# Norm products ahead of the last scores, and one exp for each block of columns, in the opening of an attention and feed-forward kernel

## Chip, cores, metric

The kernel runs on one core of a Trainium2 chip. The metric is device time in microseconds (us) of one execution, as a median over executions. "Before" is the tuned kernel, "after" the changed one. A trace is one execution taken by the hardware profiler; its span is about 2 us shorter than the device time.

## The reference, cut to what matters

```python
# q, k, v: [4, 6016, 256];  x is [24064, 256];  tau = 1
qn = q / (norm(q, axis=1) + 1e-6)          # norms over the 6016 tokens, one per column
kn = k / (norm(k, axis=1) + 1e-6)
s  = kn.T @ qn / tau                       # [256, 256] for each of 4 batches
a  = exp(s - rowmax);  a /= a.sum(-1) + 1e-9
x  = v @ a
out = (sigmoid(x @ w_gate) * (x @ w_val)) @ w_out      # 256 -> 1536 -> 256
```

## The kernel before

`v @ a` is never formed. For each batch the kernel folds the 256x256 attention matrix into the weights (`G = a @ w_gate`, `H = a @ w_val`, called the gate and val products below, twelve groups of two matmuls) and then runs a long main loop of matmuls over tokens. For batches 1 to 3 the norms and scores are worked out inside the main loop of the batch before. Batch 0 has nothing to hide behind: its path runs in the first 40 us. It is the only part that the change touches.

```python
def norms_sqrt(b):                 # ScalarE: square root of the summed squares, 128x4
def norms_inv(b):                  # VectorE: add 1e-6, reciprocal
def spread_k(b, i, pl, tag):       # TensorE: k's inverse norms along the free axis, in PSUM
def copy_s(b, j):                  # VectorE: scores from PSUM to SBUF, 128x256, for j = 0, 1

def weights(b, i):                 # block i of 128 columns
    ...
    for j in range(CB):            # CB = 2
        y = attp.tile([P, P], FP32, tag=f"y{i}{j}", name="y_sb")
        nc.vector.tensor_tensor(
            out=y, in0=s["x"][:, j, ds(i * P, P)], in1=s["rk"][i], op=ALU.mult
        )
        nc.scalar.activation(
            out=e[:, j, :], in_=y, func=ACT.Exp, bias=shift, scale=s["r"][:, j : j + 1]
        )
    ...
# ---- the opening, after the loop over the groups of q and k ----
st[0]["n"] = ps_n0
norms_sqrt(0)
nc.scalar.preload_act_table(ACT.Exp)
copy_s(0, 0)
norms_inv(0)
copy_s(0, 1)
busy(3)
spread_k(0, 0, pso, "o")
spread_k(0, 1, pso, "o")
...
weights(0, 0)
weights(0, 1)
...                                # v of the first tokens transposed by TensorE
sums(0, 0)                         # row sums of block 0, and their inverse
gh(0, 0, psg, "g", act=False)      # gate product of block 0
gh(0, 1, psv, "v", act=True)       # val product of block 0: first reader of the first val tile
sums(0, 1, pss, "s")
gh(0, 2, psg, "g", act=False)      # gate product of block 1
gh(0, 3, psv, "v", act=True)       # val product of block 1
nc.scalar.preload_act_table(ACT.Sigmoid)
gh(0, 4, pso, "o", act=False)
# ---- the main loop, first tokens ----
            for f in range(FC):
                glu(b, ci, f)
                ...
                if (b, ci) == (0, 0) and f < len(gh_order) - 5:
                    gh(0, 5 + f, pso, "o")     # f = 2 gives the eighth product
```

`gh(b, n, pool, tag, act)` takes a PSUM buffer of the pool, runs the two matmuls, and has ScalarE (`act` true, or even `n` where it isn't given) or VectorE empty it.

Of the kernel before, what the change touches and what calls it, by code (L numbers as in the profile page):

```python
# [9 lines left out]
FP32 = mybir.dt.float32  # L10
BF16 = mybir.dt.bfloat16
ACT = mybir.ActivationFunctionType
ALU = mybir.AluOpType
# [4 lines left out]
def kernel(  # L18
# [20 lines left out]
    nc = tc.nc  # L39
    P = nc.NUM_PARTITIONS  # L40
# [8 lines left out]
    CB = C // P  # L49
# [16 lines left out]
    def pool(name, bufs, **kw):  # L66
        return ctx.enter_context(tc.tile_pool(name=name, bufs=bufs, **kw))
# [4 lines left out]
    attp = pool("attp", 1)  # L72
# [14 lines left out]
    def mm(out, lhsT, rhs, start, stop, **kw):  # L87
        nc.tensor.matmul(out, lhsT=lhsT, rhs=rhs, start=start, stop=stop, **kw)  # L88
# [21 lines left out]
    t0, nt = groups0[0]  # L110
# [15 lines left out]
    shift = consts.tile([P, 1], FP32)  # L126
# [10 lines left out]
    for fg in range(NFG):  # L137
        for w, src in enumerate((moe_w_gate, moe_w_val)):
            nc.gpsimd.dma_start(
                out=w_sb[w][fg],  # L140
                in_=src.rearrange("(t p) f -> p t f", p=P)[:, :, ds(fg * FG, FG)],
# [11 lines left out]
    def score(b, t0, u):  # L153
        q_sb, k_sb = qk[b, t0]
        if t0 == 0 and u == 0:
            st.setdefault(b, {})["s"] = pss.tile([P, CB, C], FP32, tag="s", name="ps_s")
        ps_s = st[b]["s"]
        t = t0 + u
        for j in range(CB):
            mm(  # L160
                ps_s[:, j, :],
                q_sb[:, u, ds(j * P, P)],
                k_sb[:, u, :],
                start=(t == 0 and j == 0),
                stop=(t == NT - 1),
                skip_group_check=True,
            )

    def squares(b, t0, nt, which, engine, sq=None):
        src = qk[b, t0][which]  # L170
        if sq is None:
            sq = sqpool.tile([P, TPC, C], BF16, tag=f"sq{which}", name=f"sq{which}")
        if engine is nc.scalar:
            nc.scalar.activation(out=sq[:, :nt, :], in_=src[:, :nt, :], func=ACT.Square)  # L174
        else:
            engine.tensor_tensor(  # L176
                out=sq[:, :nt, :], in0=src[:, :nt, :], in1=src[:, :nt, :], op=ALU.mult
            )
        return sq

    def norm_mms(ps, sqs, nt, first, last, order=(0, 1)):

        for w in order:
            sq = sqs[w]
            for u in range(nt):
                for j in range(CB):
                    mm(
                        ps[:, w * CB + j : w * CB + j + 1],
                        sq[:, u, ds(j * P, P)],
                        ones_bf[:, 0:1],  # L190
                        start=(first and w == order[0] and u == 0 and j == 0),
                        stop=(last and u == nt - 1),
                        skip_group_check=True,
                    )
# [80 lines left out]
    def norms_sqrt(b):  # L275
        s = st[b]
        s["r"] = attp.tile([P, 2 * CB], FP32, tag="r", name="r")
        nc.scalar.activation(out=s["r"], in_=s["n"], func=ACT.Sqrt)

    def norms_inv(b):  # L280
        r = st[b]["r"]
        nc.vector.tensor_scalar(out=r, in0=r, scalar1=1e-6, scalar2=None, op0=ALU.add)
        nc.vector.reciprocal(r, r)
        if inv_tau != 1.0:
            nc.vector.tensor_scalar(
                out=r[:, :CB], in0=r[:, :CB], scalar1=inv_tau, scalar2=None, op0=ALU.mult
            )
# [8 lines left out]
    def copy_s(b, j):  # L296
        s = st[b]
        if j == 0:
            s["x"] = attp.tile([P, CB, C], FP32, tag="x", name="x_sb")
        nc.vector.tensor_copy(out=s["x"][:, j, :], in_=s["s"][:, j, :])  # L300

    def weights(b, i):

        s = st[b]
        e = attp.tile([P, CB, P], BF16, tag=f"e{i}", name=f"e_sb{i}", bufs=2)
        for j in range(CB):
            y = attp.tile([P, P], FP32, tag=f"y{i}{j}", name="y_sb")
            nc.vector.tensor_tensor(
                out=y, in0=s["x"][:, j, ds(i * P, P)], in1=s["rk"][i], op=ALU.mult
            )  # L310
            nc.scalar.activation(  # L311
                out=e[:, j, :], in_=y, func=ACT.Exp, bias=shift, scale=s["r"][:, j : j + 1]
            )
        s.setdefault("e", []).append(e)
        s.setdefault("rrow", [])

# [152 lines left out]
    def busy(n):  # L469

        ps = psg.tile([P, CH], FP32, tag="g", name="ps_busy")
        for _ in range(n):
            mm(ps, ones_bf, ones_wide, True, True)

    busy(9)
    ps_n0 = psm.tile([P, 2 * CB], FP32, tag="m", name="ps_n")
# [4 lines left out]
    last0 = len(groups0) - 1  # L481
    for g, (t0, nt) in enumerate(groups0):
        engines = (nc.vector, nc.scalar) if g < last0 else (nc.scalar, nc.vector)
        sq = [squares(0, t0, nt, w, engines[w], acc[w] if g == 0 else None) for w in range(2)]
        if 0 < g < n_acc:
            for w in range(2):
                nc.vector.tensor_tensor(out=acc[w], in0=acc[w], in1=sq[w], op=ALU.add)  # L487
        for u in range(nt):
            score(0, t0, u)
        if g < n_acc:  # L490
            busy(5)
        elif g == n_acc:
            norm_mms(ps_n0, acc, TPC, True, False)
            norm_mms(ps_n0, sq, nt, False, False)
        elif nt == TPC:
            busy(2)
            norm_mms(ps_n0, sq, nt, False, False)
        elif g < last0:
            held = (sq, nt)
        else:  # L500
            norm_mms(ps_n0, *held, False, False)
            norm_mms(ps_n0, sq, nt, False, True, (1, 0))
    st[0]["n"] = ps_n0
    norms_sqrt(0)
    nc.scalar.preload_act_table(ACT.Exp)
    copy_s(0, 0)
    norms_inv(0)
    copy_s(0, 1)
    busy(3)
    spread_k(0, 0, pso, "o")  # L510
    spread_k(0, 1, pso, "o")
    busy(1)
    weights(0, 0)
    weights(0, 1)
    late = []
    transpose_v(
# [123 lines left out]
```

## Time and profile before

| | before |
|---|---|
| device time, median of three | 830.18 us (829.69 to 830.32) |
| span of the trace | 827.9 us |
| TensorE busy | 817.6 us, 99% |
| the opening up to the first val product | 37.31 us |
| of it, what the prediction took the edit to touch | 33.17 to 37.31 us |

Read it from the top down: the busy shares name the engine, the chain that ended last says where its few idle microseconds are, and the rows in order of time say what it waits for there. The lines themselves are in the prediction.

### The profile page before, as it was taken

Reading aid. Unit: us, or ns where it says so; the run is one execution under the profiler, and the core shown is the slowest. Engines: PE = TensorE matmul, PEld = TensorE weight load, DVE = VectorE, ACT = ScalarE, POOL = GpSimd, SP = SyncE. Lnnn points to the kernel's source line nnn. Section 1 sums busy time; section 2 is a strip of 40 time slices with the busy share of each in tenths; the row PEclk is TensorE's granted clock in tenths of the full one; section 3 lists DMA queues with packets and bytes.
Section 4 is the critical chain, followed back from the end, with each engine's and each line's share of the span. In section 5 each row is a group of like instructions: output and inputs, shape, how many; then the busy total and the mean of one; then the engine's idle time right before and its main releaser. Section 6 shows DMA issues by size and latency. Waiting matters only on the chain.

```text
span 827.9 us, 13794 instructions
## 1 busy us (share of the span) xinstructions
PE 817.6 (99%) x5204; PEld 503.5 (61%) x5218; DVE 588.7 (71%) x1023; ACT 391.7 (47%) x644; POOL 83.1 (10%) x159
## 2 busy tenths in 40 slices
PE   8899999999999999999999999999999999999998
PEld 4556666665665666665575666666566566666666
DVE  6577877787667777778767777777766666666665
ACT  4654444446644444445654444444655444444442
POOL 5532100002110100000311010000000000000000
PEclk9999999999999999999999999999999999999999
DMA  9999623226846433233875352223323423322111
GB/s 210 206 202 212 112 52 90 59 54 136 154 93 118 96 89 61 53 52 87 155 139 128 81 106 57 51 64 74 64 62 63 71 52 86 68 49 70 45 36 72
DMA packets 79027, 77.19 MB, mean 93 GB/s; under 512 B 50800, under 2 KB 55920, under 8 KB 78960
## 3 DMA queue, kind: packets, MB, share of 16 engines
q0 software_dynamic: 23920, 38.81, 28.1%
q1 hardware_dynamic: 54752, 36.91, 17.6%
q8 instruction: 41, 0.67, 0.3%
q10 hardware_dynamic: 288, 0.59, 0.2%
q14 instruction: 26, 0.21, 0.1%
HBM read 78.64 MB, written 24.64 MB: 125 GB/s over the span
## 4 chain that ended last, share of the span: by engine, by line
PE 94%; DMA 4%; DVE 1%; issue 0%; POOL 0%; ACT 0%; POOLq 0%
PE ps_o L88 30%; PE ps_gate L88 29%; PE ps_val L88 29%; PE ps_s L88 4%; DMA q_sb<-in_q_dram 3%; PE ps_gh L88 2%; DMA w_val<-in_moe_w_val_dram 1%; DVE hT L424 0%; DVE sq L176 0%; PE ps_end L88 0%; ACT g_sb L423 0%; PE ps_n L88 0%; POOL k_sb L97 0%; POOL q_sb L97 0%; PE ps_tp L394 0%
## 5 line engine op out<-in xcount | busy, mean ns | idle before, releaser
L424 DVE TENSOR_TENSOR hT<-ps_val,g_sb 128x512 bf16<-128x512 f32 (+1 forms) x576 | 390.7, 679 | 205.6 <-ACT g_sb L423 201.0
L423 ACT ACTIVATE g_sb<-ps_gate 128x512 bf16<-128x512 f32 (+1 forms) x576 | 338.3, 588 | 386.0 <-PE ps_gate L88 379.7
L88 PE MATMUL ps_gate<-vT,gh_G 128*128 128x512 bf16 (+1 forms) x1152 | 337.7, 375 | 0.2
L88 PE MATMUL ps_val<-vT,gh_H 128*128 128x512 bf16 (+1 forms) x1152 | 337.5, 375 | 0.3
L88 PE MATMUL ps_o<-w_out_sb,hT 128*128 128x256 bf16 x2244 | 324.9, 273 | 0.0
L88 PEld LDWEIGHTS <-hT 128*128 128x128 bf16 x2268 | 221.0, 98 | 124.6
L88 PEld LDWEIGHTS <-gh_H 128*128 128x128 bf16 x1152 | 112.7, 98 | 131.6 <-issue 1.0
L88 PEld LDWEIGHTS <-gh_G 128*128 128x128 bf16 x1152 | 112.4, 98 | 37.8 <-DVE gh_G L379 0.4
L106 POOL DMA_DIRECT2D v_sb<-in_v_dram x48 | 25.6, 533 | 619.7 <-DMA vT<-v_sb 498.5
L450 DVE COPY out_sb<-ps_o 128x256 f32<-128x256 f32 x187 | 77.2, 413 | 12.6 <-PE ps_o L88 12.6
L88 PE MATMUL ps_s<-k_sb,q_sb 128*128 128x256 bf16 x376 | 67.0, 276 | 3.9 <-DMA k_sb<-in_k_dram 2.7
L88 PEld LDWEIGHTS <-q_sb 128*128 128x128 bf16 x376 | 37.1, 99 | 12.7 <-issue 5.0
L215 DVE TENSOR_TENSOR acc<-acc,sq 128x1024 bf16<-128x1024 bf16 (+1 forms) x66 | 44.1, 669 | 0.0
L176 DVE TENSOR_TENSOR sq<-q_sb 128x1024 bf16<-128x1024 bf16 (+2 forms) x44 | 29.3, 667 | 2.7 <-DMA q_sb<-in_q_dram 2.7
L97 POOL DMA_DIRECT2D k_sb<-in_k_dram x48 | 26.2, 545 | 17.1 <-DMA k_sb<-in_k_dram 8.1
L97 POOL DMA_DIRECT2D q_sb<-in_q_dram x48 | 26.3, 548 | 14.9 <-DMA q_sb<-in_q_dram 7.4
L176 DVE TENSOR_TENSOR sq<-k_sb 128x1024 bf16<-128x1024 bf16 (+2 forms) x34 | 22.4, 658 | 0.9 <-ACT sq L174 0.9
L88 PE MATMUL ps_busy<-ones_wide,ones_bf 128*128 128x512 bf16 x57 | 17.7, 440 | 1.7 <-DVE shift L127 1.6
L174 ACT ACTIVATE sq<-k_sb 128x1024 bf16<-128x1024 bf16 (+1 forms) x11 | 11.2, 1018 | 14.5 <-DMA k_sb<-in_k_dram 13.1
L487 DVE TENSOR_TENSOR acc<-acc,sq 128x1024 bf16<-128x1024 bf16 x16 | 11.1, 691 | 5.5 <-ACT sq L174 5.2
L88 PE MATMUL ps_gh<-w_val,e_sb 128*128 128x512 bf16 x44 | 13.4, 379 | 0.2
L88 PEld LDWEIGHTS <-e_sb 128*128 128x128 bf16 x112 | 10.2, 98 | 4.7 <-ACT e_sb L311 0.5
(67 smaller groups left out, 133.8 us busy)
## 6 DMA issues: line engine op xcount, KB each, us to landing
out_dram<-out_sb SPq DMA_DIRECT2D x44, 512.0 KB, 2.9
v_sb<-in_v_dram POOLq DMA_DIRECT2D x44, 256.0 KB, 3.8
q_sb<-in_q_dram POOLq DMA_DIRECT2D x43, 256.0 KB, 7.3
k_sb<-in_k_dram POOLq DMA_DIRECT2D x43, 256.0 KB, 8.0
out_dram<-out_sb SPq DMA_DIRECT2D x3, 384.0 KB, 2.5
w_gate<-in_moe_w_gate_dram POOLq DMA_DIRECT2D x3, 256.0 KB, 6.8
w_val<-in_moe_w_val_dram POOLq DMA_DIRECT2D x3, 256.0 KB, 7.4
w_out_sb<-in_moe_w_out_dram POOLq DMA_DIRECT2D x1, 768.0 KB, 12.7
```

The costliest lines, as they stand in the source:

```text
L88: nc.tensor.matmul(out, lhsT=lhsT, rhs=rhs, start=start, stop=stop, **kw)
L97: nc.gpsimd.dma_start(out=tl[:, :nt, :], in_=rows(src, b)[:, t0 : t0 + nt, :])
L106: nc.gpsimd.dma_start(out=v_sb[:, :nt, :], in_=rows(v, b)[:, t0 : t0 + nt, :])
L174: nc.scalar.activation(out=sq[:, :nt, :], in_=src[:, :nt, :], func=ACT.Square)
L176: engine.tensor_tensor(out=sq[:, :nt, :], in0=src[:, :nt, :], in1=src[:, :nt, :], op=ALU.mult)
L215: nc.vector.tensor_tensor(out=acc[:, :nt, :], in0=acc[:, :nt, :], in1=st[b]["sq", w][:, :nt, :], op=ALU.add)
L423: nc.scalar.activation(out=g_sb[:, :n], in_=ps_gate[:, :n], func=ACT.Sigmoid)
L424: nc.vector.tensor_tensor(out=hts[b, ci][:, f, :n], in0=ps_val[:, :n], in1=g_sb[:, :n], op=ALU.mult)
L450: nc.vector.tensor_copy(out=out_sb[:, s, :], in_=ps)
L487: nc.vector.tensor_tensor(out=acc[w], in0=acc[w], in1=sq[w], op=ALU.add)
```

## The change

Three small edits, meant to shorten the latency of batch 0. Its last norm products go ahead of its last scores, so the square root can start earlier. VectorE multiplies by both inverse norms in one pass, so that the exps need no scale of their own and one exp serves a block of 256 columns instead of two of 128. The inversion goes ahead of the first copy of the scores.

```diff
@@ weights
+        y = attp.tile([P, CB, P], FP32, tag=f"y{i}", name="y_sb")
         for j in range(CB):
-            y = attp.tile([P, P], FP32, tag=f"y{i}{j}", name="y_sb")
-            nc.vector.tensor_tensor(
-                out=y, in0=s["x"][:, j, ds(i * P, P)], in1=s["rk"][i], op=ALU.mult
-            )
-            nc.scalar.activation(
-                out=e[:, j, :], in_=y, func=ACT.Exp, bias=shift, scale=s["r"][:, j : j + 1]
-            )
+            nc.vector.scalar_tensor_tensor(
+                out=y[:, j, :],
+                in0=s["x"][:, j, ds(i * P, P)],
+                scalar=s["r"][:, j : j + 1],
+                in1=s["rk"][i],
+                op0=ALU.mult,
+                op1=ALU.mult,
+            )
+        nc.scalar.activation(out=e, in_=y, func=ACT.Exp, bias=shift)
@@ the loop over the groups of q and k
+        if g == last0:
+            norm_mms(ps_n0, *held, False, False)
+            norm_mms(ps_n0, sq, nt, False, True, (1, 0))
         for u in range(nt):
             score(0, t0, u)
 ...
-        else:
-            norm_mms(ps_n0, *held, False, False)
-            norm_mms(ps_n0, sq, nt, False, True, (1, 0))
@@ after the loop
+    norms_inv(0)
     copy_s(0, 0)
-    norms_inv(0)
     copy_s(0, 1)
```

## The prediction

> **What bounds the kernel now.** I read the page first: engines, then the chain that ended last.
>
> ```profile
> PE 817.6 (99%) x5204; PEld 503.5 (61%) x5218; DVE 588.7 (71%) x1023; ACT 391.7 (47%) x644; POOL 83.1 (10%) x159
> PE 94%; DMA 4%; DVE 1%; issue 0%; POOL 0%; ACT 0%; POOLq 0%
> ```
>
> TensorE is busy for 817.6 of 827.9 us and is 94% of the chain. The rest is mostly DMA, in the opening. The edited function runs once, for the first batch; later batches use another path, which the diff leaves alone. So I cut the span at the place where the edit works (columns: stretch, its length, then busy time and instructions of PE, PEld, DVE, ACT, POOL, the granted clock, DMA share, GB/s):
>
> ```profile
> 33.17:37.31 4.14, 3.72 (x45) 2.50 (x43) 2.93 (x12) 3.54 (x8) 3.51 (x5) 1.00 1.23 203
> 37.31:50.00 12.69, 12.64 (x59) 5.55 (x60) 9.76 (x18) 9.84 (x17) 4.17 (x8) 1.00 1.27 205
> ```
>
> Everything that the edit touches begins and ends in the 4.14 us of the first row. From 37.31 us on TensorE is dense again. Even if that whole stretch vanished, the gain would be 4.14/828 = 0.5%: a change of over 2% is out of reach by size alone.
>
> Next, the chain of waits in order of time, between 30 and 43 us (start, length, what):
>
> ```profile
> 30.47 6.80 DMA w_val<-in_moe_w_val_dram
> 37.27 0.04 issue
> 37.31 0.59 PE ps_gh L88 x2
> ...
> 42.39 0.43 PE ps_val L88 x2
> 42.83 0.51 PE ps_gh L88 x2
> ```
>
> The chain does not pass through the norms, the copies or the exps. It comes out of the load of the first val-weight tile, issued at 30.47 us and landed at 37.27, and enters TensorE at 37.31 with the product that reads that tile. Last, the same stretch instruction by instruction:
>
> ```profile
> 33.42 0.40 ACT L174 ACTIVATE sq<-q_sb 128x256 bf16<-128x256 bf16 x1
> 33.57 0.29 DVE L176 TENSOR_TENSOR sq<-k_sb 128x256 bf16<-128x256 bf16 x1 [0.87 <-ACT sq L174]
> 33.84 0.44 PE L88 MATMUL ps_n<-ones_bf,sq 128*128 128x1 bf16 x12
> 34.04 0.42 DVE L300 COPY x_sb<-ps_s 128x256 f32<-128x256 f32 x1 [0.18 <-PE ps_s L88]
> 34.32 0.17 ACT L278 ACTIVATE r<-ps_n 128x4 f32<-128x4 f32 x1 [0.50 <-PE ps_n L88]
> 34.53 0.17 DVE L282 TENSOR_SCALAR r<-r 128x4 f32<-128x4 f32 x1
> 34.73 0.18 DVE L283 RECIPROCAL r<-r 128x4 f32<-128x4 f32 x1
> 34.83 0.39 DVE L300 COPY x_sb<-ps_s 128x256 f32<-128x256 f32 x1
> 35.55 0.88 DVE L308 TENSOR_TENSOR y_sb<-x_sb,ps_rk 128x128 f32<-128x128 f32 x4 [0.33 <-PE ps_rk L88]
> 35.88 1.65 ACT L311 ACTIVATE e_sb<-y_sb,shift,r 128x128 bf16<-128x128 f32 x4
> 36.81 0.18 PE L88 MATMUL ps_r<-ones_bf,e_sb 128*128 128x1 bf16 x1 [0.21 <-ACT e_sb L311]
> 36.85 0.38 PE L88 MATMUL ps_gh<-w_gate,e_sb 128*128 128x512 bf16 x1
> 41.48 0.69 DVE L424 TENSOR_TENSOR hT<-ps_val,g_sb 128x512 bf16<-128x512 f32 x1 [1.45 <-ACT g_sb L423]
> ```
>
> Two gate products stand between 36.85 and the val product (the row shows one, a record may be missing); the products of 128x512 follow one another every 0.216 us in the dense part, so TensorE reaches the val product at 36.85 + 0.43 = 37.28 anyway. The load landed at 37.27. Latency chain and load arrive together, which is why the list of waits has no row for this load.
>
> **What the Trainium skill says.** (1) "ScalarE: Activation LUTs", section What ACT_TABLE_LOAD costs: an activation with a per-partition pointer as bias takes 280 ns + 0.833 ns per element, each further pointer operand adds 93 ns. For the present exps (128 columns, bias and scale) that gives 480 ns; the trace has a median of 478. Without the scale and with 256 columns it gives 493 ns; the later batches' exps of just that shape have 500. The trace agrees. (2) "VectorE: DVE Perf Modes", section on the TRN2 errata: a float32 two-tensor operation takes (N+151)/0.96 ns, 291 ns at 128 columns; the trace has 280. The page has no row for the fused form with a scalar, so I take that from the trace. (3) "Perfetto Trace Analysis", section Per-instruction lifecycle: VectorE and ScalarE are strict first-in first-out. That matters for the reordered copies: a copy behind the inversion can no longer use the time in which the inversion waits.
>
> **The change part by part.**
>
> *Norm products ahead of the last two scores.* Now 12 norm products follow 6 score products. The scores come every 0.112 us or so, and the last two take 0.22. In the new order the 8 held norm products can start at about 33.62. The last four must still wait for the last squares, whose VectorE part ends at 33.57 + 0.29 = 33.86; with some 0.06 us of signal they start at 33.92. Products of one column follow every 0.026 us here (the 12 span 0.44, one lasts 0.163: 0.28/11), so the last starts near 34.03 instead of 33.84 + 0.28 = 34.12. Gain at the square root: 0.09 us, not 0.22.
>
> *Inversion ahead of both copies.* Before, the first copy (34.04 to 34.46) filled the wait for the square root, and the inversion began at 34.53 only because the root ended at 34.49: the copy delayed nothing. After, both copies stand behind it. Inversion 34.44, reciprocal 34.64, first copy 34.74, second 35.13 (0.39 us each from the rows of L300), first product 35.52. The spread norms, which set 35.55 before, would be there at 35.55-0.09 = 35.46. So the 0.09 shrinks to 0.03.
>
> *One VectorE pass with both norms.* Four two-tensor operations follow one another every 0.20 us (35.55 to 36.15). The fused form is in the trace at 128x256: 474 ns each, a pair in 0.86 us, so one every 0.39. Taking off 128 columns at 0.96 GHz (0.133) gives estimates of 0.34 us for one and 0.26 us apart. Added: 4 x 0.06 = 0.24 us of VectorE time.
>
> *Two exps in place of four.* Old: starts every 0.39 us from 35.88; first block of columns complete at 36.27 + 0.48 = 36.75, second at 37.53. New, with the first product at 35.52: products 0 and 1 done at 35.52 + 0.26 + 0.34 = 36.12, exp from 36.17 to 36.67; products 2 and 3 done at 35.52 + 0.78 + 0.34 = 36.64, exp from 36.69 to 37.19. The first block comes 0.08 us earlier, the second 0.34 us; ScalarE is saved two instructions.
>
> *What reaches TensorE.* The first row sum and gate product start at 36.77 instead of 36.85; then the val product comes due at 37.20 and its tile lands at 37.27. It starts at 37.31, as before. The second block is wanted only after it, so its 0.34 us go into idle time. On VectorE the first eviction of G moves 0.08 us earlier, and with it the second, on which the first gate product of the main loop waits about 0.13 us at 39.3. That 0.08 us would be won, but at 42.74 TensorE already waits about 0.08 us for a VectorE eviction, which stands behind the row at 41.48, which stands behind a sigmoid at 40.85, the sigmoid table load at 39.55 and ScalarE's eviction of the second val block at 38.85, and that follows from 37.31. An earlier TensorE just waits longer there. Sum: 0.09 - 0.06 + 0.05 = 0.08 us on the first block, 0 to 0.08 us on the end, most likely 0.
>
> **The rivals.** *The load is no pin.* The load and the chain meet within 0.02 us, so I can't see which holds; landing times are inferred. If the tile were early, the val product would move by 0.08, the second block's 0.34 us would still be cut by TensorE's own order, and the end would move by about 0.1 to 0.3 us: 829.9. Against it speaks that the chain leads back to this very load. *The copies become the bound.* If the fused form or the copies are slower by 0.1 us each, the first block comes 0.3 to 0.5 us later, past the load, and TensorE pays it: 830.4 to 830.6. For it speaks that the margin is only 0.1 us and that VectorE keeps strict order; against it, that both durations are taken from rows of this trace. *A shift that alters the steady state.* A start moved by 0.1 us could change how the 46 transposing loads or buffer releases interlock later; for this speaks that POOL spends 498.5 us in total waiting for them. But the work after 50 us is the same instructions in the same order (the lists of the two programs differ on TensorE only around the last scores), and TensorE is 99% busy there: below 0.5 us either way.
>
> **Range and chances.** Centre: 830.2 - 0.04 = 830.1 us. The three runs of before spread over 0.63 us (829.69 to 830.32), more than any effect named. I take that spread to either side and some for another chip: 829.2 to 831.0. Chances: 0.3% faster by over 2%, 99.4% within, 0.3% slower; the 4.14 us bound is what makes the middle nearly certain.
>
> **What would show it.** Right: the val product again at 37.3 us, with TensorE now idle just before it for about 0.1 us and the load named as releaser; two exps of about 500 ns, the second ending near 37.2; the square root near 34.23; the first product of norms near 35.5, with the second copy and no longer the spread norms just ahead of it; everything from 45 us on at the same times to 0.1 us. Wrong in a step: a square root still at 34.3 (the squares were the limit), a fused product starting after 35.65 (the copies bind), or a val product before 37.2 or after 37.4. My prediction fails if the time moves by more than about 1 us, which no path that I found allows.

## The result, and the profile after

After: median 830.02 us (829.89 to 830.65, six runs). Before, with the runs of the same rounds: 829.94 us (829.69 to 830.32, six runs). The ratio is 1.0002, with a 95% interval of 0.9989 to 1.0015: the same. Ratios here are the mean time of one kernel's fast runs over that of the other's fast runs of the same rounds, so not quite the ratio of the quoted medians. Experiments with one time only have no ratio, and the state of such a run is unknown; their verdicts rest on the trace.

The page of after, engines and the chain that ended last, then the two stretches that the prediction cut out (same columns):

```profile
PE 816.0 (99%) x5204; PEld 502.8 (61%) x5218; DVE 589.5 (71%) x1023; ACT 391.0 (47%) x642; POOL 83.0 (10%) x159
PE 94%; DMA 4%; DVE 1%; ACT 0%; issue 0%; POOL 0%; POOLq 0%
```

```profile
33.17:37.31 4.14, 3.58 (x45) 2.52 (x43) 3.05 (x12) 3.33 (x7) 3.53 (x5) 1.00 1.23 203
37.31:50.00 12.69, 12.55 (x58) 5.44 (x58) 9.61 (x17) 9.28 (x15) 4.14 (x8) 1.00 1.26 205
```

ScalarE has two instructions fewer; nothing else on the page tells the kernels apart (TensorE's busy time is 817.6 and 816.9 us in the two traces of before, 816.0 and 818.1 in those of after). The rows of after in order of time do (start, length, engine, operation, in square brackets the idle time ahead of it and what ended it):

```profile
33.59 0.29 DVE L176 TENSOR_TENSOR sq<-k_sb 128x256 bf16<-128x256 bf16 x1 [0.87 <-ACT sq L174]
34.05 0.38 PE L88 MATMUL ps_s<-k_sb,q_sb 128*128 128x256 bf16 x2
34.23 0.17 ACT L278 ACTIVATE r<-ps_n 128x4 f32<-128x4 f32 x1 [0.39 <-PE ps_n L88]
34.44 0.17 DVE L282 TENSOR_SCALAR r<-r 128x4 f32<-128x4 f32 x1 [0.55 <-ACT r L278]
34.73 0.73 DVE L300 COPY x_sb<-ps_s 128x256 f32<-128x256 f32 x2
35.46 1.12 DVE L308 SCALAR_TENSOR_TENSOR y_sb<-x_sb,r,ps_rk 128x128 f32<-128x128 f32 x4
36.10 1.02 ACT L316 ACTIVATE e_sb<-y_sb,shift 128x256 bf16<-128x256 f32 x2 [0.40 <-DVE y_sb L308]
36.73 0.38 PE L88 MATMUL ps_gh<-w_gate,e_sb 128*128 128x512 bf16 x1
37.33 0.59 PE L88 MATMUL ps_gh<-w_val,e_sb 128*128 128x512 bf16 x2 [0.23 <-DMA w_val<-in_moe_w_val_dram]
```

The root is 0.09 us earlier than before, the first gate product 0.12 us. The second block of columns is complete at 36.10 + 1.02 = 37.12 instead of 37.53. All of it stops at the last row: TensorE now idles ahead of the first val product, until its load has landed, and starts it at 37.33 instead of 37.31. That is the wait that the prediction named. What follows it was not foreseen. The chain of waits of after, in order of time:

```profile
30.49 6.80 DMA w_val<-in_moe_w_val_dram
37.29 0.04 issue
37.33 0.59 PE ps_gh L88 x2
...
38.87 0.69 ACT gh_H L380
...
39.58 1.28 ACT L530
...
40.87 0.61 ACT g_sb L426
...
42.11 0.75 DVE gh_G L382
42.86 0.04 issue
42.90 0.59 PE ps_gh L88 x2
```

Before, the chain stayed on TensorE between 37.31 and 43 us. After, it leaves TensorE: ScalarE's eviction of a val product, the load of the sigmoid table, the first sigmoid, a VectorE eviction, and only then TensorE's eighth product, at 42.90 instead of 42.74.

Absolute times of different executions can't be compared to 0.1 us here: the loads of q and k shift the whole opening. VectorE's last squares (the first row above) start anywhere between 33.57 and 33.96 us in the fourteen traces. From there on the same kernel, traced twice, repeats to 0.01 us up to the main loop and 0.02 us at the end. So all traces are read from that row's start:

| us after the start of the last squares | first gate product | first val product | eighth product | first output product | last 24 products ("last group") |
|---|---|---|---|---|---|
| before | 3.28 | 3.74 | 9.17 | 20.42 | 789.61 |
| after | 3.14 | 3.74 | 9.31 | 20.57 | 789.69 |

The change wins 0.14 us up to the first gate product, loses all of it at the load, and loses another 0.15 us between there and the first output product. Half of that is made up later, near 608 us, for a reason that stays open (below).

### The profile page after: what moved, and what is told of

It is laid out like the page before. It is cut to its first block, busy times and chain, and to the rows that moved or that the text cites. A ratio compares the mean times of both kernels' runs of the same rounds, so it can differ in the third digit from the quotient of the medians.

```text
span 827.8 us, 13793 instructions
## 1 busy us (share of the span) xinstructions
PE 816.0 (99%) x5204; PEld 502.8 (61%) x5218; DVE 589.5 (71%) x1023; ACT 391.0 (47%) x642; POOL 83.0 (10%) x159
## 4 chain that ended last, share of the span: by engine, by line
PE 94%; DMA 4%; DVE 1%; ACT 0%; issue 0%; POOL 0%; POOLq 0%
PE ps_o L88 30%; PE ps_gate L88 29%; PE ps_val L88 29%; PE ps_s L88 4%; DMA q_sb<-in_q_dram 3%; PE ps_gh L88 2%; DMA w_val<-in_moe_w_val_dram 1%; DVE hT L427 0%; ACT g_sb L426 0%; DVE sq L176 0%; PE ps_end L88 0%; ACT L530 0%; PE ps_n L88 0%; DVE gh_G L382 0%; ACT gh_H L380 0%
```

## The experiments

Theory: two things hide the gain. The load of the first val tile pins the first val product (A). The build gave the eighth product the other of the two PSUM buffers of the pool `pso`, which VectorE empties later than ScalarE emptied the old one (B). Rivals: the releaser that the trace names is wrong; the loss comes from the earlier norms, or is noise.

The evidence for B ahead of the runs. Rows of before, then of after, around the eighth product:

```profile
42.00 0.69 ACT L377 ACTIVATE gh_H<-ps_gh,rrow 128x512 bf16<-128x512 f32 x1
42.09 0.74 DVE L379 TENSOR_SCALAR gh_G<-ps_gh,rrow 128x512 bf16<-128x512 f32 x1
...
42.74 0.59 PE L88 MATMUL ps_gh<-w_val,e_sb 128*128 128x512 bf16 x2
```

```profile
41.90 0.69 ACT L380 ACTIVATE gh_H<-ps_gh,rrow 128x512 bf16<-128x512 f32 x1
42.11 0.74 DVE L382 TENSOR_SCALAR gh_G<-ps_gh,rrow 128x512 bf16<-128x512 f32 x1
...
42.90 0.59 PE L88 MATMUL ps_gh<-w_val,e_sb 128*128 128x512 bf16 x2
```

Before, the product starts 0.05 us after ScalarE's eviction ends (42.69) and ahead of the end of VectorE's (42.83). After, ScalarE is done at 42.59 and the product still waits until 0.05 us after VectorE's end (42.85). In the lists of the two built programs the products around the eighth come in the same order, but the eighth has another wait:

```
before:  Matmult ps_gh<-w_val_181,e_sb_509 128x512 [waits Activation_49]
after:   Matmult ps_gh<-w_val_181,e_sb_507 128x512 [waits DVE_49]
```

These lists are not among the files of the runs; the two programs, built again from their kernel.py, have the same two waits. They also show the buffers: before, the eighth product gets the one that the seventh has just used, which ScalarE empties; after, it gets that of the sixth, which VectorE empties. The products behind it swap buffers, and some waits, accordingly.

### The two kernels once more

No edit.

> The kernel before once more, for the repeatability of the trace. Counted from VectorE's last squares: first val product 3.74, eighth product 9.17, first output product 20.42, last product group 789.61, all to 0.03 us (the last to 0.1). If they scatter by 0.15 us, the difference of 0.15 us between the two kernels in these readings is noise.

> The changed kernel once more: val product 3.74, eighth product 9.31, first output product 20.57, last group 789.69, to 0.03 us (the last to 0.1). If the eighth product is at 9.1 here, the loss through the buffer was an accident of one execution.

Measured, in the order of the table's columns: 3.27, 3.73, 9.17, 20.42, 789.61 for before; 3.13, 3.73, 9.30, 20.56, 789.67 for after. Single times were 829.82 and 830.29 us. The loads were at different places (last squares at 33.67 and 33.95), and the differences stay. So 0.13 to 0.14 us at the eighth product is a property of the two programs, not of an execution, though it drowns in the spread of the device times.

### The load taken away (results wrong)

```diff
-                w_sb[w][fg][:, j, :],
+                w_sb[0 if fg == 0 else w][fg][:, j, :],
```

The first two val products read the gate tile, which is there. The load itself is still made.

> The kernel before, with the first two val products reading the gate tile, so the load of the first val tile no longer holds them (wrong result on purpose). Theory 'the load is the pin': here the chain of latencies and the load met within 0.03 us, so almost nothing is won: first val product near 37.28 us instead of 37.31, eighth product of that group still near 42.7, the end the same to 0.1 us. Rival 'the load is no pin': no different either; this run is the base for the next.

> The changed kernel with the same wrong read. Theory 'the load is the pin': TensorE no longer idles 0.23 us, the first val product starts at 36.73 + 0.43 = 37.16 instead of 37.33, so 0.12 us ahead of the run before; the sigmoid table load and the eviction behind it move up by the same 0.17, the eighth product to about 42.73. Rival 'the trace's releaser is wrong and something else holds the val product': it stays at 37.3. Time within 0.2 us of the changed kernel either way, which rounds can't show.

The former val product started two matmuls (0.43 us) behind the first gate product in both: at 3.71 in the run of before (3.74 with the load) and at 3.56 in that of after (3.74). In the absolute times that the expectation used, 37.40 and 37.20; the last squares began 0.12 and 0.05 us later here than in the first traces. So the load held before by 0.03 us and after by 0.18, as expected. The chain of the run of after no longer goes through a load; it passes through the very steps that the change shortened:

```profile
35.51 0.61 DVE y_sb L308 x2
36.12 0.02 issue
36.15 0.52 ACT e_sb L316
...
36.91 0.89 PE ps_gh L88 x4
```

The eighth product of the run of after starts at 9.14, which is the 42.73 of the expectation. First output product: 20.43 and 20.39. Here the change is worth 0.04 us, although B is still there. Times: 829.79 us, ratio 0.9999 against before, and 830.20 us, ratio 1.0004 (interval 0.999 to 1.0017), which tell nothing, as expected.

### The eighth product in a third buffer

```diff
-                    gh(0, 5 + f, pso, "o")
+                    gh(0, 5 + f, *((pss, "s") if f == 2 else (pso, "o")))
```

`pss` has one buffer, free at that time.

> The kernel before, with the eighth product of the opening group in a third, free PSUM buffer. Theory 'which buffer it gets decides when it starts' : before, it waited for ScalarE's eviction that ends at 42.69; freed of that it starts when TensorE gets there, 42.23 + 0.43 = 42.66 instead of 42.74, so 0.08 us earlier, and what follows likewise. Rival 'TensorE is held there by something other than the buffer': stays at 42.74.

> The changed kernel with the same third buffer. Theory 'the change moved the eighth product to the buffer that VectorE evicts, whose copy ends at 42.85': it starts at 42.24 + 0.43 = 42.67 instead of 42.90, and the first output product and the end come 0.2 us earlier than in the changed kernel; against slot_before no difference beyond 0.05 us, so the change proper is worth nothing. Rival 'the 0.16 us lost there comes from the later waits of the main loop or is trace noise': 42.9 stays. Time 829.8, not separable from 830.0 by rounds.

The eighth product started at 9.10 in the run of before (9.17 without the edit) and at 9.08 in that of after (9.31), where 42.66 and 42.67 of the expectations are 9.09 and 9.08; the first output product at 20.36 and 20.33, the last group at 789.55 and 789.45. The edit is worth 0.07 us to before and 0.23 us to after, and with it the two kernels are 0.03 us apart. That settles B: which buffer the eighth product gets decides when it starts, and without that the change proper is worth almost nothing. The times, 830.04 and 829.70 us (ratios 1.0002 and 0.9999, intervals of about 0.0013 either way), order the two as the traces do but show no difference.

### Part by part

Each of these is before with only the named parts of the diff; no further edit.

> Only the norm products move ahead of the last scores; copies, inversion and exps as before. All times counted from the start of VectorE's last squares, since the loads shift the whole opening by up to 0.4 us between executions. Theory 'the reordering of the copies had to come with it': the first copy now waits for scores that end at 0.84, the inversion behind it starts near 1.24 instead of 0.96, the first product of norms at 2.26 instead of 1.98, the first gate product at 3.56, and that is past the load: first val product at 4.00 instead of 3.74, first output product of the main loop at 20.68 instead of 20.42. Rival 'moving the norm products is a gain by itself': val product at 3.74, output at 20.4.

Measured: root at 0.64, inversion at 1.22, first product of norms at 2.23, first gate product 3.53, val product 3.96, first output product 20.67; one time, 830.33 us. Moving the norm products alone costs 0.22 us at the val product, because VectorE takes its instructions in order and the first copy, ahead of the inversion, now waits for scores that come later: the root ended at 34.69 us of that trace, the copy began at 34.76, and the inversion behind it only at 35.10. The inversion had to move with them.

> Norm products and inversion moved, the four products and four exps as before. Theory: root at 0.64, first product of norms at 1.87, first gate product at 1.87 + 1.30 = 3.17, val product held by its load at 3.74. The eighth product keeps the buffer that ScalarE empties (the program lists show it), so it starts at 9.08 to 9.10, not at 9.31, and the first output product at 20.33 to 20.36: a little ahead of the kernel before (20.42) and 0.2 ahead of the whole change (20.57). Rival 'the lost 0.15 us came from the earlier norms': output at 20.57 here too.

Measured: root 0.64, first product of norms 1.87, first gate product 3.16, val product 3.74, eighth product 9.08, first output product 20.34, last group 789.46; one time, 829.74 us. These two parts keep the buffer that ScalarE empties. At the first output product they are 0.08 us ahead of before and 0.23 ahead of the whole change.

> Only the fused product and the two exps; order of norms, copies and inversion as before. Theory: first product of norms at 1.98, first gate product at 1.98 + 1.27 = 3.25, val product at 3.74; the eighth product has the buffer that VectorE empties and starts at 9.31, first output product 20.57, as with the whole change. Rival 'the loss belongs to the norms': 9.17 and 20.42.

Measured: first product of norms 1.98, first gate product 3.25, val product 3.72, eighth product 9.30, first output product 20.55; one time, 830.48 us. The fused product and the single exps bring 0.03 us at the first gate product, and they alone bring the other buffer: this is the part of the diff with which the 0.15 us are lost.

### How much slack the load leaves

```diff
+    pad = attp.tile([P, C], FP32, tag="pad", name="pad")
+    for _ in range(3):
+        nc.vector.tensor_tensor(out=pad, in0=st[0]["x"][:, 0, :], in1=st[0]["x"][:, 1, :], op=ALU.mult)
     weights(0, 0)
```

> The changed kernel with three needless VectorE products of 128x256 ahead of the products of norms, about 0.34 us each, 1.0 us in all (results stay right). Theory 'the load leaves 0.15 us of slack and no more': first gate product at 3.14 + 1.0 = 4.15, val product 0.44 behind it at 4.59 instead of 3.74, and this 0.85 us is paid in full to the end: output at 21.42, time near 830.9. Rival 'the opening has more slack than the trace shows': output moves by less than 0.5 us.

The three products took 0.43 us each and started 0.46 us apart, where the expectation had 0.34: each began only after the one before had ended (they write one tile, which would explain it; not tested). The products of norms began at 3.16 instead of 1.87, 1.29 us later. The val product came at 4.85 instead of 3.74, the first output product at 21.68 instead of 20.57, the last group at 790.80 instead of 789.69: 1.11 us later in all three. So 0.18 us of a delay goes into the wait for the load, and the rest is paid one for one to the end of the kernel. The time was 831.09 us, ratio 1.0015 (0.9998 to 1.0032). The size of the delay was mis-stated in the expectation, its law was not. The 0.18 us agree with the run without the load, from the other side.

### Both holds taken away

The edits of the two sections on the load and on the third buffer together, on after.

> The changed kernel with both holds taken away: first two val products read the gate tile (wrong on purpose), eighth product in a third buffer. Theory 'load and buffer are all that hides the gain': first output product at 20.33 - 0.17 = 20.16, that is 0.26 us ahead of the kernel before. Rival 'a further wait follows': it stays at 20.3.

First output product at 20.21, last group at 789.33; one time, 829.90 us. Of the 0.26 us expected against before, 0.21 came. The trace shows two further waits. The fifth product, first reader of the second gate tile, starts at 5.01 where TensorE would have been there at 4.91; it starts at 5.01 in the run of after without the load and in the next section's version too, which fits a landing of that tile, though no run takes this load away. Then the second matmul of the main loop's first gate product is 0.06 us late, behind a VectorE eviction.

### A version that beats both

Cut here: `gh` is split into the product and `evict`, and the list `held_gh` is made.

```diff
+    nc.scalar.preload_act_table(ACT.Sigmoid)   # was after the fourth product
     sums(0, 0)
-    gh(0, 0, psg, "g", act=False)
-    gh(0, 1, psv, "v", act=True)
+    gh(0, 0, psg, "g", act=False, late=held_gh)   # its eviction is issued after sums(0, 1)
     sums(0, 1, pss, "s")
+    evict(0, *held_gh.pop())
     gh(0, 2, psg, "g", act=False)
+    gh(0, 1, psv, "v", act=False)
     gh(0, 3, psv, "v", act=True)
-    nc.scalar.preload_act_table(ACT.Sigmoid)
-    gh(0, 4, pso, "o", act=False)
+    gh(0, 4, pso, "o", act=True)
+    gh(0, 5, pso, "o", act=False)                 # the loop goes on with the seventh
```

> A version meant to beat both, with right results: the changed kernel, but the second gate product goes ahead of the first val product (the second block of columns is ready at 3.5 now), the sigmoid table is loaded in ScalarE's idle time ahead of the last exps' evictions, VectorE takes one eviction over, and the sixth product goes ahead of the main loop. Theory: TensorE has no wait over 0.05 us from 3.63 on, first output product at 20.33 - 0.10 - 0.05 - 0.12 = 20.06 (up to 20.15 if the second gate tile is late), 0.3 us ahead of the kernel before; time 829.6 to 829.7, inside the spread of the runs. Rival 'the evictions on VectorE now hold TensorE' : a wait of 0.2 us or more at the first val product of the main loop, output at 20.3 or later.

Results right. First output product at 20.13, last group at 789.32: 0.29 us ahead of before, 0.44 and 0.37 ahead of after. TensorE's rows from the second gate product on:

```profile
37.48 0.59 PE L88 MATMUL ps_gh<-w_gate,e_sb 128*128 128x512 bf16 x2
37.91 1.03 PE L88 MATMUL ps_gh<-w_val,e_sb 128*128 128x512 bf16 x4
38.83 1.02 PE L88 MATMUL ps_gh<-w_gate,e_sb 128*128 128x512 bf16 x4
```

Groups of two follow one another every 0.43 us: the second gate product fills the time of the load, and the first val product starts at 37.91 without a wait. The third row is 0.06 us late (four products behind 37.91 would be 38.77); it is the first reader of the second gate tile, and this is the "second gate tile is late" that the expectation allowed for. Time 829.72 us (829.43 to 830.16), ratio 0.9995, interval 0.9981 to 1.0008: not shown by the clock, only by the trace.

## Why the prediction was right, and where it was not

**Outcome.** 830.1 us was predicted, 829.2 to 831.0 as the range; measured 830.02. Single times of one kernel scatter by 0.6 us and more, which is above every effect here, so the agreement of the medians does not test the steps; the traces do. "Within 2%" was safe, but the bound of 4.14 us was not strictly one: the edit also changed a wait at 42.74 us, outside that stretch, and it was luck that this cost no more than 0.15 us.

**Square root.** Right: 34.23, as predicted, because the last squares and not the scores limit it: the last four norm products start at 33.94, 0.06 us after VectorE's squares end at 33.88. The gain was 0.11 us once both traces are counted from those squares.

**Copies.** Right that they use up gain, a little too pessimistic. The first product of norms came at 35.46, not 35.52: two copies took 0.73 us from the first start to the next instruction, where 0.78 was assumed. The copies end just when the spread norms were estimated to be there, so which of the two bounds this step isn't told apart. The second rival, that the copies become the bound and the block comes late, falls: the first gate product came earlier.

**Fused product.** Right in size: 0.34 us for one and (1.12 - 0.34)/3 = 0.26 apart, both as estimated from the wider form.

**Exps.** Right: 0.507 us each where the later batches' exps had suggested 0.500. The fused pass and the exps together gained 0.03 us on the first block, where the prediction had 0.05. The first gate product came 0.14 us earlier instead of 0.08; alone, the norms and inversion bring 0.12, the fused pass and exps 0.03.

**The load.** Right, and now shown: the val product started at 37.33, the idle time ahead of it is in the trace with the load as its releaser, taking the load away moved it to 3.56, and a delay was swallowed up to 0.18 us. The first rival, that the load is no pin, falls. In before it held by only 0.03 us, which fits the list of waits having no row for it.

**The wait at 42.74.** This step failed, though what led up to it was right. The prediction said that the wait of the main loop's first gate product for VectorE would shrink, and it did: the sixth product, behind it, starts at 6.38 instead of 6.50. It said that an earlier TensorE would just wait longer behind the first sigmoid, and it does, one step ahead of the eighth product: the second val product of the main loop starts at 8.65 (before 8.66), 0.05 us after VectorE's product with that sigmoid ends. But of the wait at 42.74 it named the wrong releaser. It took it for a VectorE eviction and concluded "0 to 0.08 us on the end, most likely 0". In before it was ScalarE's eviction, 0.14 us ahead of VectorE's; the rows of both were there to be compared with the start of the product. The change moved the product to the buffer that VectorE empties, and the wait became what the prediction thought it was already. In place of "everything from 45 us on at the same times to 0.1 us" the eighth product came 0.14 us later, the first output product 0.15, the last group 0.08, all counted from the squares. The prediction had compared the order of instructions in the two programs and said that they differ "on TensorE only around the last scores"; it had not compared their waits, where the change stands.

**The third rival,** a shift that changes the later steady state, was bounded at 0.5 us. Something of the kind exists and is small: between the first output product and the last group before takes 769.19 us and after 769.12, and all fourteen traces show 769.11 to 769.20. In before one pair of val products of the main loop, at 607.99 us, stands in the chain with 0.50 us instead of 0.43; in after it does not. There VectorE starts a product 0.25 us after the sigmoid that it needs has ended (606.90 to 607.15), where 0.03 is usual. The long pair goes with the program and not with the execution: it is in all seven traces of programs with 1632 instructions for VectorE, and in none of the seven with 1633 or 1635. `p_norms` has it and `p_norms_inv` has not, and these two differ only in the place of the first copy and in one semaphore instruction on VectorE that comes with it. So it hangs on VectorE's list and not on how late the opening ends, as the version of the last section has the long pair too; why VectorE is late there stays open. How the pool decides between its two buffers is open as well: only that the decision changes with the exps, and what it costs, is shown.

## What to carry to other kernels

A latency chain and a load that arrive together are worth nothing one by one: shorten the chain and the load takes its place, so look for other work to put into the gap, as the second gate product here. Where buffers come from a pool, compare the waits of the two built programs and not only the order of their instructions, since a small edit can hand a later product a buffer that is emptied later. For differences below the spread of the times, read the traces from a common event inside them instead of from their start.

## What the Trainium skill lacked or had wrong

- "ScalarE: Activation LUTs", section What ACT_TABLE_LOAD costs, gives 2.66 us for every switch to another set, 1283 ns of load and about 1380 ns of drain. In after ScalarE's eviction ends at 39.56, the load runs from 39.58 to 40.86 and the first sigmoid starts at 40.87: 1.31 us from work to work. The load's size agrees, the drain isn't seen.
- "VectorE: DVE Perf Modes", section on the TRN2 errata, has a formula for the two-tensor operation but none for the fused form with a per-partition scalar: 0.340 us at 128x128 float32 with one input in PSUM, against 0.280 for the two-tensor operation at the same place.
- No page that was read says how far the landing of a queue of loads moves between executions of one program: the start of the last squares, which follows the loads of q and k, was 33.59 and 33.95 us in the two traces of after, further apart than the two kernels are in any column of the table.
